# Input-block sums of the first expert round: from TensorE and PSUM to GpSimd and the accumulators' tiles

## The chip, the cores and the metric

One core of a Trainium2 chip. The time is the device time of one execution in microseconds, the median of several runs. The engines work side by side and each takes its instructions in order: TensorE (matmuls, results in PSUM banks), VectorE and ScalarE (elementwise, both read PSUM and SBUF), GpSimd (elementwise, SBUF alone) and SyncE, whose queue issues the DMAs. Rows call them PE (PEld for its weight loads), DVE, ACT, POOL and SP.

## The reference, cut to what matters

Attention with a position bias gives x of 2304 tokens by 512. A mixture of eight experts follows, all of them applied to every token, with gates P from 8 rounds of row and column scaling:

```python
for e in range(E):                      # E = 8, w1[e]: 512 x 1024, w2[e]: 1024 x 512
    h = np.maximum(x @ w1[e], 0.0)
    ye = h @ w2[e]
    out += P[:, e:e + 1] * ye
```

## The kernel before, in words

Every float32 operand is kept as two half-precision parts (high and rest), and a product of two operands is three matmuls. Experts 1 to 7 multiply 2 x 2 blocks with seven products in place of eight (Winograd's form of Strassen's scheme), for the first layer (`l1`, `prod1`, line 1606) and the second (`l2`, `prod2`, line 1626). The scheme needs sums of the four quarters of an input block: T1 = B12 - B11, T2 = B22 - T1, T3 = B22 - B12, T4 = B21 - T2. B11 and the others are the quarters of the block of x, each as high plus rest.

The tokens are five blocks: four of 512 tokens (0 to 3; a product works on 256 at a time) and one of 256 (block 4; 128 at a time). An expert goes through the five blocks; a stay at a block is a visit, and the first expert of this part visits 3, 0, 1, 4, 2. Visits alternate between two sets of tiles: `xt0`, which holds the four T of even visits, with accumulators `acc0` to `acc3`, and `xt1` with `acc4` to `acc7`. The accumulators hold the output rows of the visit's tokens. When a visit ends they are stored to DRAM (`acc_done`), and those of the visit after next are loaded into them (`acc_ready`; in expert 1 ScalarE also scales them, line 1789). The T of a block are formed once, in expert 1, are stored (`sc_t`), and are loaded again by later experts. Blocks 1 to 3 pass through the tile `xc`; blocks 0 (`xa`) and 4 stay in SBUF.

For the first two visits `t_prep` forms the T on VectorE. For the other three, blocks 1, 4 and 2, `t_mm` lets TensorE add high and rest and the quarters, with the identity `id16` and its negative `nid16` as weights, into the banks S0 and S1 (line 1441); ScalarE copies each sum into `xt` as high part (line 1451) and VectorE subtracts for the rest (line 1454). `t_ready` calls it after the first layer of the visit two before.

The order on every engine is set when the program is written: `Plan` collects steps with engine, estimated cost, reads, writes and a priority, runs a list schedule on these estimates, and emits the steps in order of its start times. Changing the steps therefore changes the order around them on all engines. While expert 1 runs, the weights of expert 2 are also prepared by the same VectorE and ScalarE queues (`w_steps`; the tiles raw, xb, xc, stage), largest values are looked for by ScalarE (junk, line 1485), and the results go out by DMA (`sc_w`). In the first layer `comb` is a VectorE step that reads a bank and writes a c tile (line 1219), `snap` a ScalarE copy of a bank (p1, u2, p7, u4), and `put` makes the two half-precision parts of a hidden tile (hA, hS, area). `comb` of the bank A sum must be done before TensorE adds its next product to that bank.

Of the kernel before, what the change touches and what calls it, by code (L numbers as in the profile page):

```python
# [9 lines left out]
F16 = mybir.dt.float16  # L10
# [3 lines left out]
ALU = mybir.AluOpType  # L14
# [4 lines left out]
P = 128  # L19
B, H, S, D = 4, 8, 576, 64  # L20
# [250 lines left out]
def attention_sinkhorn_moe(ctx, tc, q, k, v, w1, b1, w2, wg, m1, m2, xm, xm4, xf, sel, out):  # L271
# [11 lines left out]
    plan = Plan()  # L283
    vec, act, pool, pe, sync = (
        Engine(plan, e, n)
        for e, n in ((nc.vector, "dve"), (nc.scalar, "act"), (nc.gpsimd, "pool"), (nc.tensor, "pe"), (nc.sync, "dma"))
    )
# [14 lines left out]
    ident = consts.tile([P, P], F32, name="ident")  # L302
    id16 = consts.tile([P, P], F16, name="id16")
# [109 lines left out]
    with ExitStack() as actx:  # L413
# [105 lines left out]
        for kind in range(1, 4):  # L519
            vec.scalar_tensor_tensor(  # L520
                out=wr,
                in0=wbs[:, kind // 2, kind % 2, :],
                scalar=selt[:, kind : kind + 1],
                in1=wr,
                op0=ALU.mult,
# [4 lines left out]
            out=wa.rearrange("p g (j k) -> p (g j) k", j=4),  # L530
            in0=wr.unsqueeze(1).broadcast_to([P, 16, HID]),
            in1=selt[:, 8:24].unsqueeze(2).broadcast_to([P, 16, HID]),
            op=ALU.mult,
# [89 lines left out]
        def bias_step(between=()):  # L623
# [27 lines left out]
            out=w1r, in0=pw[:, H : H + 2], scalar1=s_wb[:, 0:1], scalar2=2.0**-11, op0=ALU.mult, op1=ALU.mult  # L651
# [5 lines left out]
            out=w2m,  # L657
            in0=w2r.unsqueeze(2).broadcast_to([P, H, 4]),
            in1=selt[:, 4:8].unsqueeze(1).broadcast_to([P, H, 4]),
            op=ALU.mult,  # L660
# [19 lines left out]
        for i in range(2):  # L680
            r = slice(32 * i, 32 * i + 1)
# [110 lines left out]
        for n in range(8):  # L792
            for m in (2 * n, 2 * n + 1):
                nm, _, i = qk_order[m]
# [9 lines left out]
        with plan.urgent():  # L804
# [6 lines left out]
            out=c8, in0=u_qk[:, 0:1], scalar=0.125, in1=u_qk[:, 1:2], op0=ALU.mult, op1=ALU.mult  # L811
# [7 lines left out]
            out=g, in0=g0, scalar=s_qk[:, 0:1], in1=s_qk[:, 1:2], op0=ALU.mult, op1=ALU.mult  # L819
# [292 lines left out]
        for u in range(len(units)):  # L1112
            f = 5 * u
# [77 lines left out]
        vec, act, pool, pe, sync = nc.vector, nc.scalar, nc.gpsimd, nc.tensor, nc.sync  # L1191
# [7 lines left out]
    fin = ctx.enter_context(tc.tile_pool(name="fin", bufs=1, reuse_waits="tile"))  # L1199
    psB = ctx.enter_context(tc.tile_pool(name="psB", bufs=1, space=PSUM, reuse_waits="tile"))  # L1200
    bank = {f"{k}{i}": psB.tile([P, 512], F32, name=f"bank{k}{i}") for k in "ABES" for i in range(2)}
# [4 lines left out]
    def on_act(cost, fn, r, w, prio=1):  # L1206
        plan.add("act", cost, fn, r, w, prio)

    def on_vec(cost, fn, r, w, prio=1, after=0.0):
        plan.add("dve", cost, fn, r, w, prio, after)  # L1210

    def on_pe(cost, fn, r, w, prio=0):
        plan.add("pe", cost, fn, r, w, prio)

    def dma(o, i, r, w, after=4.0):
        plan.add("sp", 0.1, lambda: sync.dma_start(out=o, in_=i), r, w, 1, after)
# [14 lines left out]
    acc = [fin.tile([P, DM], F32, name=f"acc{t}") for t in range(8)]  # L1231
# [149 lines left out]
    for i in range(4):  # L1381
        tmp[f"g{i}"] = stage[i // 2][:, i % 2].bitcast(F32)
    XT = ("T1", "T2", "T3", "T4")
    nid16 = fin.tile([P, P], F16, name="nid16")
    on_vec(
        0.2,
        lambda: vec.tensor_scalar(out=nid16, in0=ident, scalar1=-1.0, scalar2=None, op0=ALU.mult),
        [],
        ["nid"],
        2,  # L1390
    )

    def t_prep(v, xk, w, dst, dk, ts):


        def whole(k, dq, tok):
            r = tmp[k][:, : 2 * w].rearrange("p (c n) -> p c n", c=2)
            x = [v[:, a, 2 * dq : 2 * dq + 2, tok * w : tok * w + w] for a in range(2)]
            on_vec(0.69, lambda: vec.tensor_tensor(out=r, in0=x[0], in1=x[1], op=ALU.add), xk, [k], 2)
            return r  # L1400

        def put(i, k, r):
            d = dst[i]
            on_act(0.52, lambda: act.copy(d[:, 0], r), [k], dk[i], 2)
            on_vec(
                0.6, lambda: vec.tensor_tensor(out=d[:, 1], in0=r, in1=d[:, 0], op=ALU.subtract), [k], dk[i], 2
            )

        def less(o, y, r, wk):
            on_vec(0.69, lambda: vec.tensor_tensor(out=o, in0=y[0], in1=y[1], op=ALU.subtract), r, wk, 2)  # L1410

        b11, b12 = whole(ts[0], 0, 0), whole(ts[1], 0, 1)
        less(b11, (b12, b11), [ts[1]], [ts[0]])
        put(0, ts[0], b11)
        b22 = whole(ts[2], 1, 1)
        less(b12, (b22, b12), [ts[2]], [ts[1]])
        put(2, ts[1], b12)
        less(b22, (b22, b11), [ts[0]], [ts[2]])
        put(1, ts[2], b22)
        b21 = whole(ts[3], 1, 0)  # L1420
        less(b21, (b21, b22), [ts[2]], [ts[3]])
        put(3, ts[3], b21)

    def t_mm(v, xk, w, dst, dk):

        terms = (
            (0, ((0, 1, 1), (0, 0, -1))),
            (2, ((1, 1, 1), (0, 1, -1))),  # L1430
            (1, ((1, 1, 1), (0, 0, 1), (0, 1, -1))),
            (3, ((1, 0, 1), (0, 1, 1), (1, 1, -1), (0, 0, -1))),
        )
        for n, (i, parts) in enumerate(terms):
            bk = f"S{n % 2}"
            r = bank[bk][:, : 2 * w].rearrange("p (c n) -> p c n", c=2)

            def fn(parts=parts, r=r):
                seq_ = [(a, *t) for t in parts for a in range(2)]
                for j, (a, dq, tok, sg) in enumerate(seq_):  # L1440
                    pe.matmul(
                        r,
                        id16 if sg > 0 else nid16,
                        v[:, a, 2 * dq : 2 * dq + 2, tok * w : tok * w + w],
                        start=(j == 0),
                        stop=(j == len(seq_) - 1),
                    )

            d = dst[i]
            on_pe(len(parts) * w / 600, fn, [*xk, "nid"], [bk])  # L1450
            on_act(0.58, lambda d=d, r=r: act.copy(d[:, 0], r), [bk], dk[i], 1)
            on_vec(
                0.69,
                lambda d=d, r=r: vec.tensor_tensor(out=d[:, 1], in0=r, in1=d[:, 0], op=ALU.subtract),
                [bk],
                dk[i],
                1,
            )

    USE = (("A11", "A12", "S2", "S3", "S1", "A22", "S4"), ("B11", "T4", "B21", "T2", "T3", "T1", "B22"))  # L1460
    scal = {e: [[s2([P, 1]) for _ in range(2)] for _ in range(2)] for e in range(1, E)}
# [122 lines left out]
    at = lambda b: b if b in (0, 4) else 3  # L1584
# [212 lines left out]
    for e in range(1, E):  # L1797
        a, b = (x for x in (1, 2, 3) if x != here)
# [3 lines left out]
    visits, visit = [], []  # L1802
# [19 lines left out]
    def t_make(b, z, ts, src):  # L1822
        x = xts(b, z)
        a = xv[src], XK[src], WID[b], [x[:, k] for k in range(4)], [[f"t{z}{k}"] for k in range(4)]
        if ts is None:
            t_mm(*a)
        else:
            t_prep(*a, ts)
        n = 16 * WID[b]
        dma(sc_t[b, :, :n], xt[z][:, :n], [f"t{z}{k}" for k in range(4)], [f"st{b}"])  # L1830

    def t_ready(r):
        if r >= len(visits):
            return
        (e, b), z = visits[r], r % 2
        if e == 1:
            t_make(b, z, None, at(b))
            return
        m = 16 * WID[b]
        dma(xt[z][:, :m], sc_t[b, :, :m], [f"st{b}"], [f"t{z}{k}" for k in range(4)])  # L1840
# [11 lines left out]
    def acc_ready(r):  # L1852
        if r >= len(visits):
            return
        (e, b), z = visits[r], r % 2
        if e == 1:
            first_part(tiles_of(b, z))
            return
        for t, a in tiles_of(b, z):
            dma(acc[a], sc_y[t], [f"y{t}"], [f"acc{a}0", f"acc{a}1"])  # L1860

    def acc_done(r, e):
        b, z = visits[r][1], r % 2
        if e < E - 1:
            for t, a in tiles_of(b, z):
                dma(sc_y[t], acc[a], [f"acc{a}0", f"acc{a}1"], [f"y{t}"])
# [18 lines left out]
    for n, (e, b) in enumerate(seq):  # L1885
        r = visit[n]
        i, at_end, leaves = (b, r % 2), n % 5 == 4, visit[n + 1 : n + 2] != [r]
        nxt = e + 1 if e < E - 1 else None
        if n % 5 == 0:
            gate_col(e)  # L1890
            if nxt:
                w_load(nxt, 1)
                w_max(nxt, 1)
                todo.extend(w_steps(nxt, 0) + w_steps(nxt, 1))
                if nxt < E - 1:
                    todo.insert(7, lambda e=nxt + 1: (w_load(e, 0), w_max(e, 0)))
                if n == 0:
                    for _ in range(3):
                        paced()
        l1(i)  # L1900
        x_ready(n)
        if leaves:
            t_ready(r + 2)
        if at_end and nxt:
            assert len(todo) <= 7
            w_fetch(nxt, 0)
        l2(i, pairs(b, r % 2), f"pcol{e}", pcols[e], e == E - 1)
        if leaves:
            acc_done(r, e)
            acc_ready(r + 2)  # L1910
        if at_end and nxt:
            assert not todo, len(todo)
            w_fetch(nxt, 1)
# [70 lines left out]
```

## Time and profile before

| | |
|---|---|
| median of 3 runs | 1766.91 us (1764.6 to 1772.89) |
| span of the profiled execution | 1765.7 us |
| TensorE busy | 1681.9 us, 95%, 16640 matmuls |
| VectorE busy | 1427.0 us, 81% |
| ScalarE busy | 1086.1 us, 62% |
| GpSimd busy | 73.9 us, 4% |

The profiled execution's own time is its span; what the runs add around it lies within their spread. The visits of expert 1 lie at about 562 to 759 us of the span. Busy shares are averages over the whole span: what a stretch is limited by is read from that stretch alone. A matmul row lists a duration with its pipeline tail, so a group's pace is read from one start to the next.

### The profile page before, as it was taken

How to read it: one execution, taken by the hardware profiler on the slowest of the kernel's cores; microseconds unless marked ns; L12 is line 12 of the kernel's file. 1: busy time of each engine (PE TensorE's matmuls, PEld its weight loads, DVE VectorE, ACT ScalarE, POOL GpSimd, SP SyncE). 2: the span in 40 equal slices, each digit the busy share in tenths (PEclk: the TensorE clock that was granted, in tenths of full speed). 3: DMA queues.
4: the chain of work that ended last, by engine and by line, in shares of the span. 5: the costliest groups of instructions: out<-in, count | busy, mean ns of one | idle time of the engine just before them, and what ended most of it. 6: DMA issues, size and time to landing. Idle time of an engine off the chain costs nothing.

```text
span 1765.7 us, 40391 instructions
## 1 busy us (share of the span) xinstructions
PE 1681.9 (95%) x16640; PEld 1374.4 (78%) x16640; DVE 1427.0 (81%) x2603; ACT 1086.1 (62%) x1930; POOL 73.9 (4%) x119
## 2 busy tenths in 40 slices
PE   7887897989999899999999999999999999999998
PEld 4554564656585688788988898889888988898887
DVE  6998989988866988678878887888788878876666
ACT  7997888888864766445554654565555644453443
POOL 0111011111002000000000000000000000000000
PEclk9998898999999999999999999999999999999999
DMA  7779899999974346545574456455654743463321
GB/s 259 245 174 241 184 211 210 216 191 210 187 236 167 120 176 215 173 142 184 179 264 151 156 203 239 158 176 194 206 189 168 253 178 132 166 236 103 103 77 37
DMA packets 290813, 322.52 MB, mean 183 GB/s; under 512 B 182972, under 2 KB 217284, under 8 KB 285636
## 3 DMA queue, kind: packets, MB, share of 16 engines
q1 hardware_dynamic: 290628, 319.94, 60.4%
q8 instruction: 130, 2.13, 0.5%
q14 instruction: 55, 0.45, 0.1%
HBM read 189.33 MB, written 88.08 MB: 157 GB/s over the span
## 4 chain that ended last, share of the span: by engine, by line
PE 82%; DVE 7%; DMA 5%; ACT 3%; issue 2%; SPq 0%; POOL 0%; DVEq 0%; ACTq 0%; POOLq 0%
PE bankA L1606 18%; PE bankA L1626 14%; PE bankB L1626 9%; PE bankE L1626 9%; PE bankE L1606 9%; PE l L210 7%; PE bankB L1606 4%; PE s L210 4%; PE pv L210 4%; PE bankA L393 2%; DMA aT<-ah 2%; ACT area L210 1%; DVE area L210 1%; DVE ah L210 1%; DVE sb L210 1%
## 5 line engine op out<-in xcount | busy, mean ns | idle before, releaser
L1606 PEld LDWEIGHTS <-slot 128*128 128x128 f16 x5040 | 451.6, 98 | 51.9 <-issue 5.3
L1626 PEld LDWEIGHTS <-hA 128*128 128x128 f16 x2268 | 221.3, 98 | 26.3 <-DVE hA L1219 0.4
L210 PEld LDWEIGHTS <-area 128*128 128x128 f16 (+1 forms) x2477 | 153.1, 100 | 99.5 <-issue 31.4
L1606 PE MATMUL bankE<-xt,slot 128*128 128x256 f16 (+1 forms) x1680 | 186.1, 262 | 2.0 <-DVE c L1219 2.0
L1651 ACT ACTIVATE hA<-c 128x512 f16<-128x512 f32 x189 | 118.3, 627 | 112.4 <-DVE c L1219 111.4
L1606 PE MATMUL bankA<-xt,slot 128*128 128x256 f16 (+1 forms) x1680 | 187.4, 263 | 0.0
L1626 PEld LDWEIGHTS <-hS 128*128 128x128 f16 x1512 | 148.0, 98 | 24.5 <-ACT hS L1651 4.5
L1626 PEld LDWEIGHTS <-area 128*128 128x128 f16 x1512 | 148.7, 98 | 21.7 <-issue 3.5
L1219 DVE SCALAR_TENSOR_TENSOR hA<-c,hA 128x512 f16<-128x512 f32 x189 | 127.4, 684 | 13.3 <-ACT hA L1651 11.1
L1710 ACT COPY u<-bankA 128x512 f32<-128x512 f32 (+1 forms) x70 | 37.8, 540 | 156.5 <-PE bankA L1626 156.5
L1663 ACT ACTIVATE u<-bankA 128x512 f32<-128x512 f32 x126 | 75.1, 596 | 72.0 <-PE bankA L1606 64.1
L210 PE MATMUL l<-area 128*128 128x512 f16 (+1 forms) x413 | 110.8, 385 | 5.5 <-ACT area L210 1.7
L210 ACT ACTIVATE sb<-sb,st 128x576 f32<-128x576 f32 x144 | 110.7, 771 | 7.9 <-DVE st L210 7.7
L1219 DVE SCALAR_TENSOR_TENSOR acc<-c,fs,acc 128x256 f32<-128x256 f32 x252 | 110.3, 479 | 2.0
L210 DVE SCALAR_TENSOR_TENSOR ah<-sb,st,ah 128x576 f16<-128x576 f32 x121 | 97.6, 831 | 15.7 <-ACT ah L210 15.7
L210 PE MATMUL s<-qkT 128*128 128x512 f16 (+3 forms) x560 | 83.3, 298 | 14.7 <-DVE st L210 14.1
L210 ACT ACTIVATE ah<-sb,st 128x576 f16<-128x576 f32 x121 | 89.5, 772 | 10.0 <-DMA aT<-ah 7.3
L1626 PE MATMUL bankA<-area,hS 128*128 128x256 f16 x756 | 89.9, 275 | 4.4 <-ACT hS L1651 3.9
L1626 PE MATMUL bankB<-area 128*128 128x256 f16 x756 | 90.1, 276 | 2.0 <-DVE area L1219 2.0
L1626 PE MATMUL bankA<-area 128*128 128x256 f16 x756 | 88.2, 273 | 1.0 <-ACT u L1710 1.0
L1626 PE MATMUL bankE<-area,hS 128*128 128x256 f16 x756 | 88.9, 273 | 0.1
L1626 PE MATMUL bankB<-area,hA 128*128 128x256 f16 x756 | 88.4, 273 | 0.2 <-DVE hA L1219 0.2
(242 smaller groups left out, 3163.4 us busy)
## 6 DMA issues: line engine op xcount, KB each, us to landing
sc_w<-stage SPq DMA_DIRECT2D x84, 512.0 KB
acc<-sc_y SPq DMA_DIRECT2D x102, 256.0 KB
area<-sc_w SPq DMA_DIRECT2D x48, 512.0 KB
sc_y<-acc SPq DMA_DIRECT2D x84, 256.0 KB
xt<-sc_t SPq DMA_DIRECT2D x18, 1024.0 KB
slot<-sc_w SPq DMA_DIRECT2D x36, 512.0 KB
bt<-sc_bias SPq DMA_DIRECT2D x26, 576.0 KB
raw<-in_moe_w_dram SPq DMA_DIRECT2D x28, 512.0 KB
```

What stands on the lines that cost most here:

```text
L210: self.plan.record(self.name, cost, lambda: fn(*args, **kw), ins, outs, move)
L393: pe.matmul(ps[:, :512], h[a][:, ft, j * P : (j + 1) * P], w[:, wl, c : c + 512], start=(ft == 0 and i == 0), stop=(ft == 7 and i == 2),)
L1219: vec.scalar_tensor_tensor(out=o, in0=x, scalar=s, in1=y, op0=op0, op1=op1)
L1606: pe.matmul(ps[:, jf * w : jf * w + w], t[:, a, c * 512 + f * P : c * 512 + f * P + P], x(xp, c), start=(first and jf == 0 and c == 0 and ...
L1626: pe.matmul(ps[:, j * 256 : j * 256 + 256], h[:, a, fc * w + j * P : fc * w + j * P + P], t[:, wp, fc * 256 : fc * 256 + 256], start=(firs ...
L1651: on_act(0.58, lambda: act.activation(h[:, 0, sl], x, AF.Relu if relu else AF.Copy), [r], wk)
L1663: on_act(0.55, lambda: act.activation(tmp[k], bank[b], f, scale=HS), [b], [k], 0)
L1710: on_act(0.27 * nt, lambda: act.copy(tmp[k][:, :n], bank[b][:, :n]), [b], [k], 0)
```

## The change

`t_pool` takes the place of `t_mm` for blocks 1, 4 and 2. GpSimd adds high and rest of the four quarters into four accumulator tiles (`whole`) and then forms the four differences in place (`less`), eight instructions for a block, 512 columns wide (256 for block 4). ScalarE and VectorE make the two parts of each T from these tiles. The tiles are those of the visit that has just ended, so the call of `t_ready` moves from behind the first layer of that visit to behind `acc_done`, its stores. The negated identity goes. Line numbers after the change are nine lower from there on, so line 1606 becomes 1597 and line 1219 stays.

```diff
-    nid16 = fin.tile([P, P], F16, name="nid16")
-    on_vec(
-        0.2,
-        lambda: vec.tensor_scalar(out=nid16, in0=ident, scalar1=-1.0, scalar2=None, op0=ALU.mult),
...
-    def t_mm(v, xk, w, dst, dk):
...
-                    pe.matmul(
-                        r,
-                        id16 if sg > 0 else nid16,
-                        v[:, a, 2 * dq : 2 * dq + 2, tok * w : tok * w + w],
...
+    def t_pool(v, xk, w, dst, dk, at):
+
+        r = [acc[a][:, : 2 * w].rearrange("p (c n) -> p c n", c=2) for a in at]
+        rk = [[f"acc{a}0", f"acc{a}1"] for a in at]
+
+        def tt(o, x, y, op, rd, wk):
+            plan.add("pool", 1.5, lambda: pool.tensor_tensor(out=o, in0=x, in1=y, op=op), rd, wk)
+
+        def whole(i, dq, tok):
+            x = [v[:, a, 2 * dq : 2 * dq + 2, tok * w : tok * w + w] for a in range(2)]
+            tt(r[i], x[0], x[1], ALU.add, xk, rk[i])
+
+        def less(o, x, y):
+            tt(r[o], r[x], r[y], ALU.subtract, rk[x] + rk[y], rk[o])
+
+        def put(k, i):
+            d, x = dst[k], r[i]
+            on_act(0.52, lambda: act.copy(d[:, 0], x), rk[i], dk[k], 1)
+            on_vec(0.7, lambda: vec.tensor_tensor(out=d[:, 1], in0=x, in1=d[:, 0], op=ALU.subtract), rk[i], dk[k], 1)
+
+        whole(0, 0, 0)
+        whole(1, 0, 1)
+        less(0, 1, 0)
+        put(0, 0)
...
         if ts is None:
-            t_mm(*a)
+            t_pool(*a, range(4 * z, 4 * z + 4))
...
-        if leaves:
+        soon = visits[r + 2 : r + 3] and visits[r + 2][0] == 1
+        if leaves and not soon:
             t_ready(r + 2)
...
             acc_done(r, e)
+            if soon:
+                t_ready(r + 2)
             acc_ready(r + 2)
```

On VectorE, at the end of the first layer of block 0, before (c220 and the others are the tiles that `comb` and `put` work on; fs38 to fs15 are the steps of a scale):

```order
L1219 SCALAR_TENSOR_TENSOR c220_6772<-bankA0_6756,p7_6766 128x512
L1219 SCALAR_TENSOR_TENSOR c111_6771<-c111_6771,u4_6767 128x512
L1219 SCALAR_TENSOR_TENSOR c211_6775<-c211_6775,s2_6769 128x512
L1219 SCALAR_TENSOR_TENSOR hA11_6794<-c110_6770,hA11_6794 128x512
L1657 TENSOR_TENSOR hS3_6798<-c111_6771,hS3_6798 128x512
L1219 SCALAR_TENSOR_TENSOR hA22_6796<-c220_6772,hA22_6796 128x512
L1657 TENSOR_TENSOR area_101<-c211_6775,area_101 128x512
L1219 SCALAR_TENSOR_TENSOR c210_6774<-bankE0_6760,u2_6765 128x512
L1219 SCALAR_TENSOR_TENSOR s1_6768<-c220_6772,u4_6767 128x512
L1504 COPY fs38_6849<-bankS1_6763 128x1
```

and after:

```order
L1219 SCALAR_TENSOR_TENSOR hA11_6794<-c110_6770,hA11_6794 128x512
L1648 TENSOR_TENSOR hS3_6798<-c111_6771,hS3_6798 128x512
L1219 SCALAR_TENSOR_TENSOR hA22_6796<-c220_6772,hA22_6796 128x512
L1436 TENSOR_TENSOR xt0_6810<-acc0_6786,xt0_6810 128x512
L1648 TENSOR_TENSOR area_101<-c211_6775,area_101 128x512
L1436 TENSOR_TENSOR xt0_6810<-acc1_6787,xt0_6810 128x512
L1219 SCALAR_TENSOR_TENSOR c210_6774<-bankE0_6760,u2_6765 128x512
L1219 SCALAR_TENSOR_TENSOR s1_6768<-c220_6772,u4_6767 128x512
L1436 TENSOR_TENSOR xt0_6810<-acc2_6788,xt0_6810 128x512
L1219 SCALAR_TENSOR_TENSOR hA12_6795<-c210_6774,hA12_6795 128x512
```

Three subtractions into xt0 now stand ahead of the hA12 step, and the six scale steps have gone behind it.

On SyncE's queue, near the end of block 1 (visit 2 stores, xt1 is loaded for a visit of expert 2), before:

```order
L1216 DMA xb_73<-in_moe_w2_dram 128x4x256
L1216 DMA sc_y_71<-acc2_6788 128x512
L1216 DMA sc_y_71<-acc3_6789 128x512
L1216 DMA sc_w_6814<-stage1_6816 128x2048
L1216 DMA xc_74<-in_moe_w2_dram 128x4x256
L1216 DMA sc_y_71<-acc0_6786 128x512
L1216 DMA sc_y_71<-acc1_6787 128x512
L1216 DMA acc2_6788<-sc_y_71 128x512
L1216 DMA acc3_6789<-sc_y_71 128x512
L1216 DMA acc0_6786<-sc_y_71 128x512
L1216 DMA xt1_6811<-sc_t_6813 128x4096
L1216 DMA acc1_6787<-sc_y_71 128x512
```

and after:

```order
L1216 DMA sc_y_71<-acc0_6786 128x512
L1216 DMA sc_y_71<-acc1_6787 128x512
L1216 DMA xt1_6811<-sc_t_6813 128x4096
L1216 DMA sc_w_6814<-stage0_6815 128x2048
L1216 DMA xb_73<-in_moe_w2_dram 128x4x256
L1216 DMA sc_w_6814<-stage1_6816 128x2048
L1216 DMA xc_74<-in_moe_w2_dram 128x4x256
L1216 DMA acc0_6786<-sc_y_71 128x512
L1216 DMA acc1_6787<-sc_y_71 128x512
L1216 DMA acc2_6788<-sc_y_71 128x512
L1216 DMA sc_t_6813<-xt0_6810 128x4096
L1216 DMA acc3_6789<-sc_y_71 128x512
```

Two weight loads (xb and xc from in_moe_w2) have moved from before the load of xt1 to behind it, and all loads of accumulators stand behind these.

On ScalarE at that place (junk is the scan of a weight tile, hA, hS and area are hidden tiles), before:

```order
L1485 ACTIVATE junk_6846,fs36_6847<-xb_73 128x1024
L1651 ACTIVATE hA11_6794<-c111_6771 128x512
L1663 ACTIVATE u2_6765<-bankA1_6757 128x512
L1485 ACTIVATE junk_6846,fs36_6847<-xc_74 128x1024
L1651 ACTIVATE hA12_6795<-c211_6775 128x512
L1710 COPY p1_6764<-bankA0_6756 128x256
L1651 ACTIVATE hA22_6796<-c221_6773 128x512
L1789 ACTIVATE acc2_6788<-acc2_6788,fs39_6850 128x512
```

and after:

```order
L1476 ACTIVATE junk_6845,fs36_6846<-xb_73 128x1024 x2
L1701 COPY p1_6764<-bankA0_6756 128x256
L1642 ACTIVATE area_101<-s1_6768 128x512
L1642 ACTIVATE hS2_6797<-s2_6769 128x512
L1642 ACTIVATE hS3_6798<-c111_6771 128x512
L1476 ACTIVATE junk_6845,fs36_6846<-xc_74 128x1024
L1435 CAST xt0_6810<-acc0_6786 128x512
```

The last scan of xb has moved from ahead of the hA11 step of this layer to right ahead of p1, area and hS2, the scan of xc from ahead of hA12 to behind hS3, and no scaling of an accumulator is left among them.

## Rows read from the trace of the kernel before

**Rows 1.** Busy time by stretch: us, engines (instructions), granted clock, DMA share, GB/s.
```profile
core 0: us, PE busy (x) PEld busy (x) DVE busy (x) ACT busy (x) POOL busy (x), PEclk, DMA share, GB/s
...
621.00:637.00 16.00, 15.05 (x134) 12.93 (x133) 15.02 (x31) 12.38 (x23) 0.00 (x0) 1.00 0.30 107
...
654.00:674.00 20.00, 20.00 (x184) 17.76 (x182) 18.85 (x37) 12.54 (x22) 0.00 (x0) 1.00 0.56 189
...
711.00:724.00 13.00, 10.00 (x64) 7.26 (x63) 4.86 (x10) 3.64 (x8) 0.00 (x0) 0.74 0.05 19
```

**Rows 2.** Groups of instructions, PE, 585 to 700: count, busy us, mean ns, idle before.
```profile
L1441 PE MATMUL bankS<-xc,id 128*128 128x512 f16 x24 | 6.5, 379 | 1.3 <-DVE xt L1454 1.3
L1441 PE MATMUL bankS<-xc,nid 128*128 128x512 f16 x20 | 5.6, 379 | 0.0
...
L1441 PE MATMUL bankS<-xa,id 128*128 128x256 f16 x12 | 2.0, 273 | 0.0
L1441 PE MATMUL bankS<-xa,nid 128*128 128x256 f16 x10 | 1.7, 273 | 0.0
```

**Rows 3.** Timeline of PE: start us, duration us, group, idle before and its releaser.
```profile
592.07 1.02 PE L1441 MATMUL bankS<-xc,id 128*128 128x512 f16 x4 [1.32 <-DVE xt L1454]
...
595.60 4.34 PE L1626 MATMUL bankB<-area 128*128 128x256 f16 x23 [1.97 <-DVE area L1219]
```

**Rows 4.** Timeline of PE, 641 to 651.
```profile
642.51 1.03 PE L1441 MATMUL bankS<-xc,id 128*128 128x512 f16 x4
...
644.24 2.78 PE L1626 MATMUL bankE<-area,hS 128*128 128x256 f16 x24
```

**Rows 5.** Timeline of POOL, 556 to 566.
```profile
557.34 0.43 POOL L1298 TENSOR_TENSOR lg<-lg,fs 128x144 f32<-128x144 f32 x1 [1.17 <-DVE fs L1295]
...
565.28 1.25 POOL L1298 TENSOR_TENSOR lg<-lg,fs 128x144 f32<-128x144 f32 x1 [0.99 <-DVE fs L1295]
```

**Rows 6.** Timeline of POOL, 212 to 229.
```profile
212.71 2.33 POOL L210 COPY qkT<-qkT 64x576 uint32<-64x576 uint32 x2 [21.39 <-ACT qkT L210]
227.85 1.39 POOL L210 COPY qkT<-qkT 64x576 uint32<-64x576 uint32 x2 [12.81 <-ACT qkT L210]
```

**Rows 7.** Groups of instructions of POOL, whole span.
```profile
L210 POOL COPY vs<-vs 64x64 uint32<-64x64 uint32 x14 | 5.5, 389 | 0.8
```

**Rows 8.** Timeline of DVE beside rows 5 and 6.
```profile
213.30 2.35 DVE L210 SCALAR_TENSOR_TENSOR ah<-sb,st,ah 128x576 f16<-128x576 f32 x2
...
565.06 1.19 DVE L1219 SCALAR_TENSOR_TENSOR stage<-raw,fs,stage 128x1024 f16<-128x1024 f32 x1
```

**Rows 9.** Groups of instructions on the page, DVE.
```profile
L210 DVE SCALAR_TENSOR_TENSOR ah<-sb,st,ah 128x576 f16<-128x576 f32 x121 | 97.6, 831 | 15.7 <-ACT ah L210 15.7
```

**Rows 10.** Timeline of SyncE's queue, 618 to 625.
```profile
619.14 3.04 SPq L1216 DMA_DIRECT2D sc_y<-acc  x4
622.27 1.98 SPq L1216 DMA_DIRECT2D acc<-sc_y  x4
```

**Rows 11.** Timeline of DVE, 621 to 637.
```profile
621.36 0.47 DVE L1219 SCALAR_TENSOR_TENSOR acc<-c,fs,acc 128x256 f32<-128x256 f32 x1
...
628.71 0.68 DVE L1219 SCALAR_TENSOR_TENSOR c<-bankA,p 128x512 f32<-128x512 f32 x1
```

**Rows 12.** Timeline of PE, 628 to 638.
```profile
629.45 1.47 PE L1606 MATMUL bankA<-xa,area 128*128 128x256 f16 x12 [0.95 <-DVE c L1219]
```

**Rows 13.** Chain of waits in order of time, 685 to 725: start us, us, what.
```profile
706.90 7.53 DMA acc<-sc_y
```

**Rows 14.** Timeline of PE, 707 to 725.
```profile
716.02 3.04 PE L1626 MATMUL bankA<-area,hS 128*128 128x256 f16 x12 [2.88 <-ACT hS L1651]
...
723.15 1.47 PE L1626 MATMUL bankA<-area 128*128 128x256 f16 x12
```

**Rows 15.** Timeline of ACT, 704 to 708.
```profile
705.38 1.06 ACT L1485 ACTIVATE junk<-xc 128x1024 bf16<-128x1024 f32 x1 [2.13 <-DMA xc<-in_moe_w_dram]
```

**Rows 16.** Groups of instructions on the page, ACT.
```profile
L1651 ACT ACTIVATE hA<-c 128x512 f16<-128x512 f32 x189 | 118.3, 627 | 112.4 <-DVE c L1219 111.4
```

More of the change, by code (lines that the diff above doesn't have):

```diff
@@ L1383, in attention_sinkhorn_moe @@
     XT = ("T1", "T2", "T3", "T4")
-    nid16 = fin.tile([P, P], F16, name="nid16")
-    on_vec(
-        0.2,
-        lambda: vec.tensor_scalar(out=nid16, in0=ident, scalar1=-1.0, scalar2=None, op0=ALU.mult),
[L1388 to L1391, printed above, removed]
     def t_prep(v, xk, w, dst, dk, ts):
@@ L1422, in t_prep @@
         put(3, ts[3], b21)
-    def t_mm(v, xk, w, dst, dk):
[L1428 to L1440, printed above, removed]
-                    pe.matmul(
-                        r,
-                        id16 if sg > 0 else nid16,
-                        v[:, a, 2 * dq : 2 * dq + 2, tok * w : tok * w + w],
[L1445 to L1458, printed above, removed]
@@ new lines, in t_pool @@
+    def t_pool(v, xk, w, dst, dk, at):
[16 more added lines that the diff above has]
+        put(0, 0)
+        whole(2, 1, 1)
+        less(1, 2, 1)
+        put(2, 1)
+        less(2, 2, 0)
+        put(1, 2)
+        whole(3, 1, 0)
+        less(3, 3, 2)
+        put(3, 3)
```

## The prediction

> **What bounds the kernel now.** I read the table of stretches first: TensorE's share by stage, since a few microseconds taken from it are worth only what that stage lets through. From 604 us on TensorE has no idle time to speak of: 20.00 of 20 us in 654 to 674, at the full granted clock, the 2.4 GHz level [rows 1]. VectorE stands right behind it: 15.02 of 16 us in 621 to 637, 18.85 of 20 in 654 to 674. The exceptions are 711 to 724, where TensorE is busy 10.00 of 13 us and the mean granted clock is 0.74, and the time before 600, where TensorE waits for VectorE [rows 1, 3]. So in the stretch that the change touches there are two engines near their limit. Taking work from TensorE pays as long as VectorE is not made slower, and GpSimd did nothing here before.
>
> **What is removed.** The page's groups give 24 + 20 matmuls of 512 columns and 12 + 10 of 256 [rows 2]: 22 for each of the three blocks, 66 in all. Their pace, not their listed duration, counts: the eight that start at 642.51 are followed by the next product at 644.24, so 0.217 us each [rows 4], and 0.109 for half as many columns. That is 44 x 0.217 + 22 x 0.109 = 11.9 us of TensorE. Not all of it is on the path. The first ten (2.2 us), of which the last six begin at 592.07, stand where TensorE waits for VectorE either way: 1.32 us for an xt tile and then 1.97 us for the weights (area) that VectorE forms [rows 3]. There only the VectorE subtraction that no longer stands ahead of those weights counts, one step of 0.6 us [rows 11]. So the gain is 11.9 - 2.2 + 0.6 = 10.3 us. The twelve ScalarE copies and twelve VectorE subtractions into xt stay; they read SBUF in place of PSUM. The small negated identity costs 0.2 us at a place where nothing waits.
>
> **What is added.** 24 GpSimd instructions with two SBUF inputs, 16 of 512 columns and 8 of 256. The trace has none of this size. The same operation on 144 columns takes 0.43 us [rows 5]; scaled with no fixed part that is 1.53 us for 512. A copy of 576 columns, one input, takes 1.39 / 2 = 0.70 us [rows 6], and two inputs of 512 columns are 1.78 times as many elements: 1.24 us. I take 1.3, near both rows, and half of it for 256 columns. From below the copy itself (0.7) bounds it; from above the dearest row per column, a copy of 64 columns in 389 ns [rows 7]: 6.1 ns a column, 3.1 us for 512.
>
> **What GpSimd does to VectorE.** The row at 565.28 took 1.25 us against 0.43 for the same line undisturbed [rows 5]: VectorE was in an instruction with two SBUF inputs from 565.06 to 566.25, and GpSimd ended 0.28 us after that [rows 8]. So 0.28 of its 0.43 us had to wait for VectorE, and 0.15 did not. It goes the other way too: two GpSimd copies took 2.33 us at 212.71 and 1.39 us at 227.85 [rows 6], and the two VectorE instructions beside the slow pair took 2.35 us [rows 8] where one has a mean of 831 ns [rows 9]: some 0.35 us lost for each copy. The Trainium skill, in SBUF — State Buffer, Who interferes with whom, says more: a VectorE instruction with two SBUF inputs and a GpSimd instruction that reads SBUF exclude each other for the whole instruction. By that rule each sum would hold VectorE for its full 1.3 us and the loss below would be 8 x 0.15 = 1.2 us larger; the rows show an overlap at the edges, and the working goes by them: 1.3 - 0.15 = 1.15 us held for 512 columns.
>
> **Block 1 (the first chain of eight).** The sums are formed in accumulators 0 to 3, so they wait until block 3's results have been stored. The stores go out at 619.14 to 622.18, and the first load back, which needs its store landed, could go at 622.27 [rows 10]. GpSimd can therefore start at about 621.2. VectorE is nearly without a gap there. Where both want the port they take turns: one VectorE step of 0.6, one GpSimd hold of 1.15, and only VectorE's steps that read a bank go beside a hold. Eight turns are 8 x 1.75 = 14.0 us. In the kernel before, the same VectorE steps, from the accumulation at 621.36 to the end of the bank A step at 628.71, thirteen of them, took 629.3 - 621.4 = 7.9 us, 0.6 each [rows 11]. VectorE is 6.1 us late at that bank A step, and TensorE waits for exactly it before it may write bank A again: today 0.95 us at 629.45 [rows 12]. So 6.1 us of wait are added. A wait of such length lowers the granted clock: after today's 1.97 us wait 23 matmuls take 4.34 us where 24 take 2.78 at the full clock [rows 3, 4]. I add the difference for 23, 1.7 us. Three xt subtractions are now ahead of the hA step that the third product waits for (1.8 us), against six small steps that move behind it (1.0 us), and TensorE has a product of the next block (1.3 us) to do meanwhile: nothing more. Together 7.8 us.
>
> **Block 4.** Eight instructions of 256 columns hold VectorE for about 4 us in all while it is busy 18.85 of 20 us [rows 1]. Two products of block 4 (24 matmuls of 128 columns, 1.3 us each) now stand between those of block 1's second layer and give VectorE that much more time: 0 to 3 us, and I take 0.5.
>
> **Block 2.** Today the place costs 6.1 us: ScalarE's in-order queue waits for an accumulator that lands 7.53 us after its issue at 706.90 behind a 1 MB load of xt; TensorE waits 2.88 us; and the 36 matmuls from 716.02 to 723.15 take 7.1 us in place of 3.9, the clock being low [rows 13, 14]. In the new order the accumulators' loads and scalings come later, but two weight loads and the scans (junk) of them have come behind the same 1 MB load of xt, which waits for TensorE to leave the first layer of block 4. If these land 7.5 us after that point, as that row has it, ScalarE needs 1.1 for the scan and 1.8 for three steps of 0.6 [rows 15, 16] and VectorE 0.6, 11.0 us in all, while TensorE has five products (60 matmuls of 256 columns or as much), 6.6 us, before it needs the hS tile. That is a wait of 4.4, with 3.2 for the clock 7.6 us: 1.5 worse than today. The GpSimd chain is done in the same time (stores landed, then 8 x 1.3 to 1.75 us, against some 16 us until the first product with xt) and is hidden here; without that cover it would cost its excess one for one.
>
> **Sum.** 10.3 - 7.8 - 0.5 - 1.5 = 0.5 us gained. The profiled execution spans 1765.7 us, 1.2 below the median of 1766.91; I take the difference from the median: 1766.4 us, no change. By the rule of the Trainium skill's page SBUF — State Buffer, named above, it would be 1767.6.
>
> **Rivals.** (1) GpSimd's holds are short or fall beside VectorE's bank steps, and the queue stall at block 2 goes without a successor. With 0.7 us an instruction, 0.55 held, eight turns are 9.2 us, 1.3 us late; the gain is 10.3 - 1.3 + 6.1 = 15, 1752 us; with today's stall kept, 1758. For it: the change leaves TensorE the only full engine, and the longest present stall is an accident of queues. Against: rows 6 and 8. Chance 0.22, all of it faster by over 0.5%. (2) The slower side: the two-input sum of half-precision slices in two pieces is slow, 3.1 us at the upper bound. One turn is then 3.55 us, eight are 28 us, and the first chain ends at 650 with VectorE 20 us late; TensorE loses 14 us more than above and block 2's sums come some 7 us late: 1787 us. It decides as soon as an instruction is over about 2 us. For it: the dear row per column; against: that row is mostly start-up. Chance 0.14. (3) The in-order queues get worse than worked out: accumulators' loads of block 4 stand behind the 1 MB load of xc on the queue, and ScalarE's hA step stands behind their scaling. With a landing at 7.5 us in place of 5 it costs 3 to 6 us more with the clock: 1771, within 0.5%, and with the same at block 2 1776. Chance 0.14, a third of it slower. (4) The change does nothing because VectorE sets the pace: the 11.9 us vanish into waits for it, at about 1767; with my forecast this holds the remaining 0.50.
>
> **Chances and range.** 0.5% is 8.8 us, about what a measurement here can tell from no change. Faster 0.22 (the first rival), slower 0.14 + 0.05 = 0.19, same 0.59. The forecast's own range is 1759 to 1775. 8 in 10 reach from 1753 into the first rival to 1780 into the second.
>
> **What would show it.** In the new profile: no bankS matmuls with id; 24 GpSimd rows, 1.3 us or up to 1.8 beside VectorE; VectorE's two-input steps of 1.2 to 1.7 us in three stretches of 9 to 14 us; a wait of 5 to 8 us of TensorE for the c step in the first layer of block 0; a ScalarE wait for a weight load near the end of block 4, with a clock below 0.9 after it. I am wrong if VectorE's steps keep 0.6 us beside GpSimd, if TensorE shows no new wait there, or if a GpSimd instruction exceeds 2 us.

## The result, and the profile after

The changed kernel took 1774.7 us in the median of 6 runs (1771.23 to 1777.24), the kernel before 1767.64 us in its 6 beside them: the two medians differ by 7.1 us, and the ratio on record is 1.0059 [1.0042, 1.0076], which is 10.4 us. It is slower by some 7 to 10 us, clear of zero; I had forecast no change, at 1766.4. The median still lies at the upper end of my range, 1759 to 1775, but a change of this size is what I had not foreseen.

The profiled execution spans 1769.4 us, 3.7 more than the one of before. The table of stretches of the changed kernel, with the columns of [rows 1]:

```profile
585.00:604.00 19.00, 13.04 (x107) 10.86 (x105) 17.40 (x21) 11.74 (x18) 0.00 (x0) 0.91 0.17 43
621.00:637.00 16.00, 9.33 (x68) 7.36 (x66) 15.00 (x17) 7.41 (x14) 9.17 (x6) 0.79 0.02 6
654.00:674.00 20.00, 19.34 (x177) 17.01 (x175) 18.09 (x30) 13.81 (x23) 8.31 (x8) 1.00 0.43 169
697.00:711.00 14.00, 11.97 (x166) 11.05 (x163) 13.38 (x18) 7.78 (x13) 4.26 (x3) 1.00 1.02 354
711.00:724.00 13.00, 5.61 (x35) 4.10 (x36) 6.20 (x10) 6.94 (x14) 7.17 (x6) 0.74 0.35 123
```

Two stretches have lost most of TensorE's work: 621 to 637, from 15.05 us busy to 9.33 with the granted clock at 0.79 in place of 1.00, and 711 to 724, from 10.00 to 5.61. In both GpSimd (the last pair of counts, in us) is at work; in 621 to 637 VectorE is as busy as before, 15.00 us, but with 17 instructions in place of 31. Half the instructions in the same busy time suggest that VectorE is held; its timeline below shows it. TensorE's waits from 580 to 760 say where that ends (us in total, times, longest). The third line, 5.2 us, is not a loss: it stands where the first ten matmuls stood.

```profile
PE bankA L1597 <- DVE c L1219: 8.1, 3, 6.7
PE bankA L1617 <- ACT hS L1642: 7.2, 1, 7.2
PE bankB L1617 <- DVE area L1219: 5.2, 1, 5.2
...
PE bankA L1617 <- DVE hS L1648: 1.6, 1, 1.6
```

**Block 1's sums.** GpSimd's and VectorE's timelines show the turns, and TensorE's what waits for them; it answers [rows 11, 12]:

```profile
618.27 2.45 POOL L1424 TENSOR_TENSOR acc<-xc 128x512 f32<-128x512 f16 x2 [42.10 <-DMA sc_y<-acc]
621.89 2.72 POOL L1424 TENSOR_TENSOR acc<-xc 128x512 f32<-128x512 f16 x2 [1.17 <-DVE c L1219]
624.57 6.72 POOL L1424 TENSOR_TENSOR acc<-acc,acc 128x512 f32<-128x512 f32 x4
```

```profile
621.79 0.68 DVE L1219 SCALAR_TENSOR_TENSOR c<-bankB,p 128x512 f32<-128x512 f32 x1
622.39 1.21 DVE L1219 SCALAR_TENSOR_TENSOR hA<-c,hA 128x512 f16<-128x512 f32 x1
623.51 1.64 DVE L1219 SCALAR_TENSOR_TENSOR s<-c,u 128x512 f32<-128x512 f32 x1
625.08 1.75 DVE L1219 SCALAR_TENSOR_TENSOR hA<-c,hA 128x512 f16<-128x512 f32 x1
626.75 1.75 DVE L1219 SCALAR_TENSOR_TENSOR s<-c,s 128x512 f32<-128x512 f32 x1
628.42 1.75 DVE L1648 TENSOR_TENSOR area<-s,area 128x512 f16<-128x512 f32 x1
...
631.76 0.68 DVE L1219 SCALAR_TENSOR_TENSOR c<-bankA,p 128x512 f32<-128x512 f32 x1
```

```profile
559.00 1.47 PE L1597 MATMUL bankA<-xc,slot 128*128 128x256 f16 x12
...
632.49 2.72 PE L1597 MATMUL bankA<-xa,area 128*128 128x256 f16 x12 [6.67 <-DVE c L1219]
635.14 0.58 PE L1259 MATMUL bankS<-fs,ones 1*128 1x1 f32 x2
635.65 3.21 PE L1617 MATMUL bankA<-area,hA 128*128 128x256 f16 x24
...
716.82 0.61 PE L1617 MATMUL bankA<-area,hS 128*128 128x256 f16 x2 [7.16 <-ACT hS L1642]
719.00 2.32 PE L1617 MATMUL bankA<-area,hS 128*128 128x256 f16 x10 [1.57 <-DVE hS L1648]
721.11 1.85 PE L1617 MATMUL bankE<-area,hS 128*128 128x256 f16 x12
```

In the kernel before, such steps start 0.6 us apart:

```profile
625.81 0.69 DVE L1219 SCALAR_TENSOR_TENSOR hA<-c,hA 128x512 f16<-128x512 f32 x1
626.42 0.69 DVE L1219 SCALAR_TENSOR_TENSOR s<-c,s 128x512 f32<-128x512 f32 x1
```

In the changed kernel VectorE starts one step per GpSimd sum from 623.51 to 630.09, every 1.57 to 1.67 us. The step at 621.79, which reads a bank and only one tile, keeps 0.68 beside GpSimd. So the c step that frees bank A comes at 631.76 and TensorE waits 6.67 us for it; the twelve matmuls after that start at about half pace (2.72 us listed in place of 1.47).

**Block 2's place.** ScalarE's timeline and the chain of waits, for the wait of 7.16 us:

```profile
707.20 0.20 ACT L1476 ACTIVATION_READ_ACCUMULATOR junk<-xb 128x1 f32 x1
714.31 1.06 ACT L1476 ACTIVATE junk<-xb 128x1024 bf16<-128x1024 f32 x1 [6.91 <-DMA xb<-in_moe_w_dram]
```

```profile
705.09 9.14 DMA xb<-in_moe_w_dram
...
716.28 1.00 DVE area L1648
717.27 1.68 DVE hS L1648
```

ScalarE, which takes its steps in order, stands behind a scan whose weights land 9.14 us after their issue, and then VectorE's two steps toward hS take 1.00 and 1.68 us, since GpSimd's last two sums stand beside them.

To compare executions I use one stretch in all that follows: from expert 1's first product to expert 2's first. Ahead of it the order is that of before, and where it begins differs by some microseconds from one execution to the next (559.00 here, 561.84 in the first profile of before). It took 203.25 us here against 197.26 in that profile: 6.0 us lost.

### The profile page after: what moved, and what is told of

It is laid out like the page before. It is cut to its first block, busy times and chain, and to the rows that moved or that the text cites. A ratio compares the mean times of both kernels' runs of the same rounds, so it can differ in the third digit from the quotient of the medians.

```text
span 1769.4 us, 40309 instructions
## 1 busy us (share of the span) xinstructions
PE 1669.6 (94%) x16574; PEld 1367.9 (77%) x16574; DVE 1436.8 (81%) x2602; ACT 1086.0 (61%) x1930; POOL 105.3 (6%) x143
## 4 chain that ended last, share of the span: by engine, by line
PE 80%; DVE 9%; DMA 5%; ACT 4%; issue 2%; SPq 0%; POOL 0%; DVEq 0%; ACTq 0%; POOLq 0%
PE bankA L1597 18%; PE bankA L1617 13%; PE bankB L1617 9%; PE bankE L1617 9%; PE bankE L1597 8%; PE l L210 7%; PE bankB L1597 4%; PE s L210 4%; PE pv L210 3%; PE bankA L393 2%; ACT area L210 2%; DVE ah L210 1%; DVE area L210 1%; DVE sb L210 1%; DMA aT<-ah 1%
## 5 line engine op out<-in xcount | busy, mean ns | idle before, releaser
L1617 PEld LDWEIGHTS <-area 128*128 128x128 f16 x1512 | 148.7, 98 | 24.5 <-issue 6.7
L1617 PE MATMUL bankA<-area,hS 128*128 128x256 f16 x756 | 89.9, 275 | 10.1 <-ACT hS L1642 8.2
L1597 PEld LDWEIGHTS <-area 128*128 128x128 f16 x840 | 75.9, 98 | 19.3 <-issue 10.5
```

Source lines behind the costliest of these rows:

```text
L1597: pe.matmul(ps[:, jf * w : jf * w + w], t[:, a, c * 512 + f * P : c * 512 + f * P + P], x(xp, c), start=(first and jf == 0 and c == 0 and ...
L1617: pe.matmul(ps[:, j * 256 : j * 256 + 256], h[:, a, fc * w + j * P : fc * w + j * P + P], t[:, wp, fc * 256 : fc * 256 + 256], start=(firs ...
```

## The experiments

Each ran beside the kernel before on its chip; "stretch" is the one just defined.

| run | median us | ratio to before | stretch us |
|---|---|---|---|
| before, first profile | 1766.91 | | 197.26 |
| before again, e12 | 1761.79 (one run) | | 192.73 |
| changed kernel | 1774.7 | 1.0059 [1.0042, 1.0076] | 203.25 |
| e1 changed again | 1773.67 | 1.0055 [1.0033, 1.0076] | 203.47 |
| e2 one column | 1765.0 | 1.0003 [0.9986, 1.0019] | 195.29 |
| e3 xt late | 1771.05 | 1.0039 [1.0024, 1.0053] | 200.65 |
| e4 not block 1 | 1763.78 | 1.0001 [0.9988, 1.0014] | 192.06 |
| e5 before, xt late | 1762.04 | 0.9984 [0.9969, 1.0000] | 190.84 |
| e6 block 2 only | 1765.19 | 1.0006 [0.9991, 1.0021] | 193.94 |
| e7 copies | 1762.77 (one run) | | 195.98 |
| e8 scans later | 1754.76 | 0.9950 [0.9931, 0.9968] | 191.58 |
| e9 scans later, all | 1765.06 | 0.9998 [0.9982, 1.0014] | 200.3 |
| e10 scans later, 2 | 1756.85 | 0.9951 [0.9934, 0.9969] | 192.52 |
| e11 scans later, 4 and 2 | 1756.59 | 0.9953 [0.9935, 0.9971] | 194.82 |

In e9 one product of expert 2 (1.31 us) stands ahead of the last ones of expert 1, so its stretch runs to the end of those, 201.63 us, less that product. A stretch is read from one execution, a ratio from several.

**e1, the changed kernel again.** No edit.

> The changed kernel again, as the base for the runs beside it and as a second profile. Theory A (GpSimd's turns hold VectorE in the first chain of sums, and at block 2 ScalarE's queue waits for a weight load that lands late behind the load of xt) expects the same three stalls of TensorE: 6 to 7 us for the c step, 6 to 9 us before the hS product, median 1772 to 1778 us. If the stalls differ by more than 2 us from the first profile, the spread of the times comes from them.

The stalls came again within 0.3 us: 6.85, 7.38 and 1.36 us. In two executions on two occasions the program stalls at the same places for the same time.

**e2, GpSimd's work taken away, its place kept.**

```
-  pool.tensor_tensor(out=o, in0=x, in1=y, op=op)
+  pool.tensor_tensor(out=o[:, :, :1], in0=x[:, :, :1], in1=y[:, :, :1], op=op)
```

> Each of the 24 GpSimd sums forms only its first column of each half (2 columns for 512 or 256); the rest of the sums is left out, the order of all engines is that of the changed kernel. Theory A (the turns on VectorE): TensorE's wait for the c step falls from 6.7 us to 1 or less and the slow clock behind it goes, 7.8 us in all; the second wait at block 2 (1.6 us, hS) goes; about 1 us at block 4. Together about 10 us below the changed kernel, 1764 to 1766, while ScalarE's wait for the xb load stays at 5 to 9 us. Rival B (the later place of the sums and the planner's new order cost the time, not GpSimd's work): within 2 us of the changed kernel, 1773 to 1777.

The ratio fell by 0.52%, 9 us, the stretch by 8.2. TensorE's timeline at the c step:

```profile
628.64 1.47 PE L1597 MATMUL bankA<-xa,area 128*128 128x256 f16 x12 [0.95 <-DVE c L1219]
```

It is the 0.95 us of before to the digit [rows 12], and the twelve matmuls are back at 1.47. The wait for hS on VectorE fell from 1.57 to 0.21, the wait behind the scan stayed (7.71 us). The order on all engines is that of the changed kernel, so most of the loss is the sums' work and not the order; rival B falls. What is left, a stretch 2.0 us shorter than in the first profile of before with 9.7 us of exposed matmuls gone, is for the most part the queue's stall.

**e3, one load moved on the queue.** In `t_ready` the load for the visit after next also waits, in the plan alone, for the accumulators' stores, and its call moves behind them. In the trace this load is the only instruction whose place differs; the other engines keep their order.

```
-  dma(xt[z][:, :m], sc_t[b, :, :m], [f"st{b}"], ...)
+  late_ = [f"y{t}" for t, _ in tiles_of(visits[r - 2][1], z)] if r == 5 else []
+  dma(xt[z][:, :m], sc_t[b, :, :m], [f"st{b}"] + late_, ...)
...
-  soon = visits[r + 2 : r + 3] and visits[r + 2][0] == 1
+  soon = r == 3 or visits[r + 2 : r + 3] and visits[r + 2][0] == 1
```

> The changed kernel, with the 1 MB load of xt for expert 2 put behind the two weight loads and the accumulators' stores on the queue; every other engine has its order unchanged. Theory A (queue order at block 2): ScalarE's wait for the xb load falls from 6.9 us to 2 to 3.5, TensorE's before hS from 7.2 to 2 to 4: 3 to 5 us gained, about 1770 to 1772, with the 6.7 us wait for the c step as before. Rival C (the DMA engines are full there, whatever stands first): the load still takes 8 us or more, less than 1.5 us gained.

ScalarE's timeline and TensorE's:

```profile
710.10 1.06 ACT L1476 ACTIVATE junk<-xb 128x1024 bf16<-128x1024 f32 x1 [2.87 <-DMA xb<-in_moe_w_dram]
```

```profile
712.62 0.39 PE L1617 MATMUL bankA<-area,hS 128*128 128x256 f16 x2 [3.12 <-ACT hS L1642]
714.95 2.31 PE L1617 MATMUL bankA<-area,hS 128*128 128x256 f16 x10 [1.94 <-DVE hS L1648]
```

The weights land 6.37 us after issue instead of 9.14, and the waits are as theory A had them; the gain is 2.8 us in the stretch, 2.6 in the medians, just under its range. TensorE's wait for VectorE's hS grew from 1.57 to 1.94: where the queue stalls less, the turns show more.

**e4, block 1 back on TensorE.** `t_mm` of before for block 1, `t_pool` for blocks 4 and 2.

> Block 1's sums go back to TensorE, at their old place; blocks 4 and 2 stay on GpSimd. The planner's order follows from that, and has both weight loads ahead of the load of xt. Theory A: the c wait falls to about 1 us with the clock (7.8 us gained), 2.6 us of matmuls come back, and 3 to 5 us are gained at block 2: about 1765 (1763 to 1768). Rival B (the later place of the sums costs the time): blocks 4 and 2 still have it, so about 1772 to 1776.

1763.78 us, 9.9 below e1: theory A, whose sum counts block 1 and block 2 together, since both weight loads also move ahead of the load of xt. At block 1's place the c wait is the old 0.95. But at block 2 2.90 us of TensorE's wait are now for VectorE's hS step beside block 2's sums.

**e5, only the load moved, in the kernel before.** The edit of e3 in the kernel before.

> The kernel before, with nothing but the 1 MB load of xt for expert 2 put behind the accumulators' loads and stores on the queue: all sums on TensorE. Theory A (queue order): the last accumulator lands some 4 to 5 us after its issue in place of 7.5, ScalarE's wait for it falls from 3.55 us to 1 or less, TensorE's wait of 2.88 us and the slow clock behind it go for the most part: 4 to 6 us below the kernel before. Rival C (the DMA engines are full there): under 1.5 us gained.

TensorE has no wait of hS left in its timeline, as A expected, but the gain was 2.2 us in the medians (ratio 0.9984), not 4 to 6. e12, below, shows why: the stall that the edit takes away was smaller there, and against e12 the stretch is 1.9 us shorter.

**e6, only block 2 on GpSimd**, with the edit of e3.

> Only block 2's sums on GpSimd (blocks 1 and 4 on TensorE as before), with the load of xt for expert 2 put late as in e3. Theory A: no new c wait in block 0; 4.75 us of matmuls go; the hS steps beside GpSimd's eight sums cost 2 to 3 us of TensorE's wait with some slow clock, about as much as the old stall of 6.1 us: 3 to 6 us below the kernel before. Rival B (the later place of the sums costs the time): block 2 is where the later place is tightest, so no gain, 0 to 4 us above the kernel before.

No gain: 1.0006, within the range of rival B and not of A. Four waits of 0.72, 2.01, 0.92 and 0.46 us for hA, hA, hS and a ScalarE copy of a bank, with a granted clock of 0.81 over 706 to 724, ate the 4.75 us of matmuls. VectorE's steps there take the 1.75 us of a step beside a sum:

```profile
708.79 1.75 DVE L1219 SCALAR_TENSOR_TENSOR hA<-c,hA 128x512 f16<-128x512 f32 x1
```

So it is theory A's mechanism that shows, at a larger price. Against e5, which has the same late load and all sums on TensorE, the stretch is 3.1 us longer and the median 3.2 us higher. No run takes the sums' work away with block 2 alone on GpSimd, so what the later place adds here stays open.

**e7, copies in place of sums.**

```
-  pool.tensor_tensor(out=o, in0=x, in1=y, op=op)
+  pool.tensor_copy(o, x)
```

> Each of the 24 GpSimd sums is replaced by a copy of its first operand, the second is left out; order unchanged. It prices the one-input operation at this size. If the port is held for two-input operations only, VectorE's steps beside the copies keep 0.6 to 0.7 us and the c wait is 1 us or less. If it is held for one-input copies as well, as the rows of before suggest (0.35 us lost for 0.7 us of copy), VectorE's steps take about 1.0 to 1.3 us and the c wait is 2 to 4 us.

VectorE's timeline beside the copies, and TensorE's:

```profile
619.59 1.09 DVE L1219 SCALAR_TENSOR_TENSOR s<-c,u 128x512 f32<-128x512 f32 x1
620.61 1.09 DVE L1219 SCALAR_TENSOR_TENSOR hA<-c,hA 128x512 f16<-128x512 f32 x1
```

```profile
625.40 1.47 PE L1597 MATMUL bankA<-xa,area 128*128 128x256 f16 x12 [2.73 <-DVE c L1219]
```

A turn with a copy takes 1.02 us, and the c wait is 2.73. One-input GpSimd work holds VectorE as well, for most of its own duration: 0.42 us of turn beside a copy that takes 0.61 alone, 1.07 beside a sum that takes 1.15 to 1.26.

**e8, a longer guess for the landing of weights**, in e5. ScalarE's scans of the weights of experts 2 and on are planned 8 us after the load, not 4.

```
   dma(raw[w][q]..., src..., [], [f"raw{w}{q}"],
+      8.0 if e > 1 else 4.0,
   )
```

> The kernel before with the load of xt put late as in e5, and with 8 us in place of 4 as the planner's guess for the landing of the weights of experts 2 and 3, so that it places their scans and scalings later on ScalarE and VectorE. Theory A (ScalarE's in-order queue stands behind scans whose loads land 6 to 10 us after issue): ScalarE's waits for xb and xc go below 1 us each and 2 to 5 us more than e5 are gained. Rival: the scales then come late for the weights' splits, and the same time is lost at the start of the next expert: within 2 us of e5.

The version that beats both: 0.9950, 0.34% (6 us) beyond e5, more than the 2 to 5 us expected. The stretch is no shorter than in e5; the gain lies behind it. From 760 us on, TensorE's whole list of waits is two lines:

```profile
PE bankA L1627 <- ACT hS L1652: 1.1, 1, 1.1
PE bankA L1627 <- DVE hS L1658: 0.3, 1, 0.3
```

In e5 the same list has eleven waits, 7.5 us in all, and ScalarE waits 33.3 us there for weight loads ahead of its scans; in e8 it waits for none.

**e9, e10, e11, the change on top of e8:** all three blocks, block 2 alone, blocks 4 and 2 on GpSimd.

> The changed kernel (all three blocks on GpSimd) with the two edits of e8: the load of xt put late and 8 us as the planner's guess for the weights' landing. Against e8 (1754.8, ratio 0.995) it shows what the change costs once the queue's stall is out. Theory A: block 1 costs 7.8 less 2.6 of matmuls, block 4 about nothing, block 2 gains 4.75 of matmuls against 4 to 5 us of hS wait and slow clock: 4 to 6 us above e8, 1759 to 1761, with the c wait of 6 to 7 us as the largest. Rival D (VectorE sets the pace, so every GpSimd turn is lost one for one in all three blocks, some 20 us of holds against 9.7 us of matmuls): 8 to 12 us above e8, 1763 to 1767.

> As e9, with only block 2's sums on GpSimd. Theory A: 4.75 us of matmuls go, 2 to 5 us of hS and hA waits with slow clock come: within 3 us of e8, 1752 to 1757. Rival D: 8 holds of 1.1 us against 4.75 us: 3 to 5 us above e8, 1758 to 1760.

> As e9, with blocks 4 and 2 on GpSimd and block 1 on TensorE. Theory A: no c wait in block 0; block 4's matmuls (2.4 us) against as much waiting, block 2 as in e10: within 3 us of e8, 1752 to 1757. Rival D: 5 to 8 us above e8, 1760 to 1763.

The whole change costs 0.48% (8.4 us) against e8, which is in rival D's range of 8 to 12 us and not in theory A's 4 to 6. With block 2 alone, or blocks 4 and 2, the ratio is that of e8 within some 3 us, as A had it and not as D (the stretches are 0.9 and 3.2 us longer, in one execution each).

The c wait of 6 to 7 us that I had expected in e9 as the largest isn't there (the longest for that bank is 0.39 us): the planner now has TensorE begin the second layer ahead of that c step, and at this place it waits for hA:

```profile
628.60 2.72 PE L1618 MATMUL bankA<-area,hA 128*128 128x256 f16 x16 [2.73 <-DVE hA L1219]
```

At block 2 its waits in e9 add up to 7.0 us (2.57, 3.85, 0.61), behind VectorE's steps beside the sums. So e9 against e11, 0.45% or 7.9 us (5.5 us in the stretch), is not the price of block 1 alone: the order elsewhere moved with it. In e10 VectorE's timeline shows what ate block 2's 4.75 us of matmuls, and TensorE's the wait:

```profile
709.39 1.75 DVE L1692 TENSOR_TENSOR area<-s,area 128x512 f16<-128x512 f32 x1
711.06 1.75 DVE L1692 TENSOR_TENSOR hS<-s,hS 128x512 f16<-128x512 f32 x1
```

```profile
712.86 2.04 PE L1661 MATMUL bankA<-area,hS 128*128 128x256 f16 x10 [3.60 <-DVE hS L1692]
```

**e12, the kernel before again.** No edit.

> The kernel before again, for a second profile. In the first the stretch from expert 1's first product to expert 2's first took 197.26 us and what follows 1006.6; in the two profiles of the changed kernel they took 203.3 and 203.5, and 1007.2 and 1008.8. If the loss lies in that stretch alone, it takes 197 us again (within 0.5), and what follows lies between 1006 and 1010 whichever kernel it is. If the changed order costs later as well, what follows stays below 1007.

The stretch took 192.73 us, not 197: the first expectation missed, and the miss is worth more than a hit. The chain of waits shows the landing of the accumulator, then TensorE's timeline the place of [rows 14] and that of [rows 3]:

```profile
705.07 4.96 DMA acc<-sc_y
```

```profile
711.62 0.39 PE L1626 MATMUL bankA<-area,hS 128*128 128x256 f16 x2 [1.49 <-ACT hS L1651]
712.35 1.27 PE L1626 MATMUL bankA<-area,hS 128*128 128x256 f16 x10 [0.34 <-DVE hS L1657]
```

```profile
593.06 2.67 PE L1626 MATMUL bankB<-area 128*128 128x256 f16 x23 [1.97 <-DVE area L1219]
```

The accumulator landed 4.96 us after its issue, not 7.53; the wait was 1.83 us with no slow clock behind it. The stall of 6.1 us that I had charged to the kernel before was one execution's; which of the two sizes is the usual one, two profiles can't tell. What follows the stretch took 1008.0 us against 1006.6 in the first profile and 1007.2 and 1008.8 in those of the changed kernel: no later loss can be told from that.

## Why the prediction was wrong, step by step

In the first pair of profiles the stretch lost 5.99 us where my sum had it gain 0.5. From start to start of the same products, measured against predicted (of the exposed matmuls 3.9 us were measured by themselves, the other 5.8 are set at their pace, and what is missing there is block 4's loss):

| step | predicted | measured |
|---|---|---|
| first ten matmuls, VectorE subtraction | -0.6 | 0.0 |
| exposed matmuls of the T sums | -9.7 | -9.7 |
| block 1: c wait, then clock | +6.1 + 1.7 | +5.9 + 1.9 |
| block 4 | +0.5 | +2.4 |
| block 2's place | +1.5 | +5.6 |
| sum | -0.5 | +6.0 (rows rounded) |

Of the 6.5 us between the two sums, block 2's place holds 4.1, block 4 1.9 and the first ten matmuls 0.6.

**Removed: right.** Where matmuls stood exposed they gave back what their pace said: the second layer around [rows 4] went from 19.62 to 15.72 us (two first-layer products that now stand in it left out), 3.90 less, for 12 x 0.217 + 12 x 0.109 = 3.9. The 0.6 us at the first ten didn't come: VectorE now waits for ScalarE's splits there (0.31 and 0.32 us) in place of subtracting.

**The chain of block 1: right**, in mechanism and size. GpSimd's sums took 1.15 to 1.26 us alone (1.3 predicted) and 1.6 to 1.7 beside VectorE, the turn 1.67 (1.75), the wait 6.67 us (0.95 + 6.1). e2 takes the work away and the wait goes; e7 shortens the work and the wait shrinks with it. VectorE's steps with one operand in a bank run through (0.68 us), those with two tiles are held. That a VectorE instruction with two SBUF inputs contends with a GpSimd instruction that reads SBUF, and one with at most one such input does not, is what the Trainium skill's page SBUF — State Buffer, Who interferes with whom, says; the trace agrees. That the two alternate one for one, with an overlap of 0.1 to 0.2 us a turn, is what the trace adds.

**The step that failed: "The GpSimd chain is done in the same time ... and is hidden here".** At block 2 I asked whether the sums would be done in time, and they were. I didn't ask, as I had at block 1, whom they hold meanwhile. VectorE's hS steps take their turns with the same eight sums: 1.57 us of wait in the changed kernel, 1.94 in e3, 2.90 in e4, 3.60 in e10. With the work taken away (e2) the wait is 0.21. The clearer the queue, the more the turns cost, until they eat the matmuls saved: 4.75 us of them bring nothing in e6 and e10.

**The queue at block 2: right place, too small.** I had ScalarE stuck behind the scan of a weight load behind the load of xt, and a wait of 4.4 us with 3.2 of clock. The wait was 7.16, since the load landed 11.1 us after xt's issue (703.11 to 714.23) where I took 7.5: this term of the sum was mis-sized most. Four stores of the accumulators and a store of weights' parts were also on the way, and the 16 DMA engines were full from 697 to 711, as in the kernel before (share 1.02 and 0.98). e3 moves the load of xt away and the landing falls from 9.14 to 6.37 us after issue; what part the stores have in the rest is not shown. The clock cost 1.8 us: 24 matmuls from 716.82 to 722.80, less the wait, in place of 24 x 0.109. Two small waits, 0.69 and 0.78 us, came too. The median is near my third rival's 1776, but that is luck: it priced accumulators that land late at blocks 4 and 2. At block 4 one did land late, 6.41 us after its issue, and ScalarE waited 4.65 us for it, but TensorE only 0.34.

**Block 4: too small.** Of the 2.4 us, three waits make up 1.77 (0.66 for a c step, 0.77 for a ScalarE copy of a bank, 0.34 for hA); I had relied on the two products that move in between to give VectorE time. What makes up the other 0.6 us is not shown.

**The baseline.** The stretch of before took 197.26 us in the profile I read and 192.73 in e12. So the gain I set against the losses, a present stall of 6.1 us that goes, was only partly there: that stall cost 1.8 us in e12. Against e12 the changed kernel loses 10.5 us in the stretch, against the first profile 6.0; the differences of the medians are 7.1 us and, in the runs beside e1, 10.1.

My tests of the steps came out: 24 GpSimd rows of up to 1.87 us, long VectorE steps, the c wait, the ScalarE wait for a weight load with the clock at 0.74 after it. They were all signs of losses I had priced (and the clock was at 0.74 there before, too); none asked for VectorE's steps at block 2.

## What to carry to other kernels

In this kernel work given to GpSimd was paid for by VectorE, one for one, wherever VectorE's steps read two tiles; ask at every place where the sums run which of VectorE's steps stand beside them and who waits for those, not only whether the sums are done in time. A stall behind a transfer, seen in one profile, can be one execution's number: look at a second profile before counting its end as a gain. Here an in-order queue waited for loads that landed later than the planner's guess, and mending the guess (e8) was worth more than moving the arithmetic.

## What the runs showed of the hardware

The granted clock did not follow the length of a wait alone. After the same wait of 1.97 us at the same place, 23 matmuls took 4.34 us in the first profile of before [rows 3], with a mean granted clock of 0.91 over 585 to 604, and 2.67 in e12, with 1.00, the 2.4 GHz level, over 583 to 602. A wait of 1.83 us in e12 left the next twelve at full pace, one of 2.88 us in the first profile didn't [rows 14]. So the 1.7 and 3.2 us that I charged for the clock are what one execution paid, and that block 1's clock came out near 1.7 (1.9) is partly luck.
